# Three of eight pairs of ff tiles of one input stage computed by seven block products

## The chip, the core and the metric

The kernel runs on one core of a Trainium2 chip. The metric is the device time of that core in microseconds, from the start of a launch to its end; below, times without a unit are microseconds. The engines named are PE (TensorE, which does the matmuls, with its own weight loads), DVE (VectorE), ACT (ScalarE) and POOL (GpSimd). SP issues DMA transfers, and POOL issues some too.

## The reference

Two computations follow each other. First, attention over 4 batches, 8 heads, 768 positions, head dimension 64: each query sees the keys less than 16 positions away, and besides them 24 summary keys, the maximum over each block of 32 keys, whose values are the means of the blocks.

```
k_sum = k.reshape(B, H, nb, block, D).max(axis=3)      # block = 32, nb = 24
v_sum = v.reshape(B, H, nb, block, D).mean(axis=3)
scores_all = concat(where(|i - j| < 16, scale * q @ k.T, -1e9), scale * q @ k_sum.T + log(block))
a = softmax(scores_all);  attn = a @ concat(v, v_sum)
```

Second, its output, laid out as 3072 tokens of 512 features, goes through a two-layer network with 2048 hidden features:

```
h = x @ w_in                            # (3072 x 512) @ (512 x 2048)
g = h * (1 / (1 + exp(-1.702 * h)))
out = g @ w_out                         # (3072 x 2048) @ (2048 x 512)
```

## The kernel before

The four batches are handled one after another, each as two halves of 384 tokens, u = 2b and 2b + 1. For the batches b = 1, 2 and 3 the main loop has two stages.

In the *input stage*, PE multiplies the transposed tokens xT with w_in. A hidden feature tile ("ff tile") has 128 of the 2048 features, so that there are 16 in each half, or 8 pairs. A plain ff tile is four matmuls of 128 x 384 (one for each 128 of the 512 input features) into one PSUM tile; ACT takes the tile through the gelu into gT, the operand of the next stage. The profile names these matmuls `ph<-xT,w_in_sb`.

In the *output stage*, gT is multiplied with w_out. Six token tiles of the batch are taken as three pairs a, b and c (class `Pair`, from line 855), and each pair is computed as a 2 x 2 block product with seven products in place of eight (a scheme of the Strassen and Winograd kind), p1 to p7. It needs sums of the blocks of gT (`sums`, three two-input operations on DVE over up to eight pairs of ff tiles; the second one overwrites block a21, which p7 reads as its weights) and sums of w_out's blocks, made once. The products stand in an order written out by hand: p1 of a, then a7, a2, a6, b1, a5, b7, a3, a4, b6, b2, b5, c1, b3, c7, c6, c2, c5, b4, c3, c4. A table, `meets`, says behind which product a step of the next batch's attention (scores, values, transposes of its output) is put. Between the products, `held` copies a PSUM tile to an SBUF tile t, and DVE adds give rows of the output, which SP stores.

Batch 3, the last, also uses seven products in its *input* stage, for the last five of its eight pairs of ff tiles (`ff_in_pairs`, line 702). There the 2 x 2 blocks are the two ff tiles of a pair and two halves of the 512 input features on the side of w_in (a11 to a22), and the halves of the input features and the two halves of the tokens on the side of xT (b11 to b22). A product M1 to M7 is two matmuls of 128 x 384, so that a pair takes 14 matmuls instead of 16. The products accumulate in PSUM: M1's result is copied into Y (line 737), where M2 is added, while its own place X receives M6, M5 and M3 in turn; M7's is held in SBUF (tile m7) and added by DVE to what M6 and M5 leave. Y[0] and Y[1] are the two halves of one PSUM tile, `big[0]`; L, the place of plain tiles (`plain`, line 773) in between, is in `big[1]`. The sums of w_in's blocks (`win_weights`, line 689, four DVE operations for each pair, tile wsum) are made during batch 2's input stage, and those of xT (four operations of 128 x 768, tile xsum) at the start of the last stage.

Every engine issues its instructions in the order in which the program writes them: a helper (line 28) keeps it, and for that reason all rows of the profile name line 28 and are told apart by their tiles. The input stages of batches 1 and 2 also carry work for the next batch, hung behind numbered ff tiles in the tables `first` and `second` (the loop from line 1150): the transposing DMAs on SP's queue that bring keys (kx) and queries (qT); `rest_k`, which reduces the keys to block maxima (ks) and copies halos and maxima into the key rows kx; `v_odd` (line 143), copies within the value rows; `bring`, which computes block sums of the values on PE (ps_vs), copies them (vs), and issues four halo and two sum DMAs on POOL's queue; and `pairs[...].sums`.

Of the kernel before, what the change touches and what calls it, by code (L numbers as in the profile page):

```python
# [35 lines left out]
def kernel(  # L36
# [103 lines left out]
            pool.dma_start(out=w5[:, j, 0, :, 0:D],  # L140
                           in_=v[b, :, j * 128:(j + 1) * 128].rearrange("h p d -> p h d"))

    def v_odd(b):
        for p in range(NP):
            r = rows_of(b % 2, p)
            dve.tensor_copy(out=r[:, :, 1], in_=r[:, :, 0])

    ident = consts.tile([128, 128], BF16, name="ident")
    make_identity(nc, ident)
# [233 lines left out]
    def key_rows(p, s, ks, eng=dve, j0=0):  # L383
        flat = flat_kx(p, s)
        n = NJ - j0
        eng.tensor_copy(out=at(flat, 256 * j0 + 64, [[256, n], [64, 2], [1, nb]]),
                        in_=ks.unsqueeze(1).unsqueeze(1).to_broadcast([128, n, 2, nb]))
# [196 lines left out]
                     in_=rows["q", b][:, 2 * g:2 * g + 2].rearrange("p i j h d -> p (i j h d)"),  # L584
                     transpose=True)

    def rest_k(p, s):
        ks = attp.tile([128, nb], BF16, name="ks", tag="ks")
        dve.tensor_reduce(out=ks.rearrange("p (j e n) -> p j e n", e=2, n=2),
                          in_=at(flat_kx(p, s), 0, [[256, NJ], [192, 2], [block, 2], [1, block]]),  # L590
                          axis=AX.X, op=ALU.max)
        key_halos(p, s)
        key_rows(p, s, ks)

    def tq1(p, eng):
        copy(eng, qT[p][1], trans(rows["q", 1][:, p].rearrange("p j h d -> p j (h d)")))
# [17 lines left out]
    def mask_now():  # L614
        while due:
            due.pop(0)()
# [69 lines left out]
    WI = 5  # L686
    wt = {}

    def win_weights(i0, i1):

        if i0 == 0:
            w = w_in_sb.rearrange("p k (i e c) -> p e k i c", e=2, c=128)[:, :, :, NI - WI:]
            wt.update({(e, h): w[:, e, 2 * h:2 * h + 2] for e in range(2) for h in range(2)})
            wt["s"] = stage.tile([128, 4, 2, WI, 128], F16, name="wsum", tag="kf")
        o, i = [wt["s"][:, n, :, i0:i1] for n in range(4)], slice(i0, i1)
        a11, a12, a21, a22 = (wt[e, h][:, :, i] for e in range(2) for h in range(2))
        dve.tensor_add(o[0], a21, a22)
        dve.tensor_sub(o[1], o[0], a11)
        dve.tensor_sub(o[2], a11, a21)
        dve.tensor_sub(o[3], a12, o[1])  # L700

    def ff_in_pairs(u, early):

        (b11, b21), (b12, b22) = xTT
        xs = castp2.tile([128, 4, 2, HALF], F16, name="xsum", tag="kb")
        t = [xs[:, m] for m in range(4)]
        big = [psb.tile([128, 1024], F32, name="pw_in", tag="big") for _ in range(2)]
        mm = [pmm.tile([128, 512], F32, name="px_in", tag="mm") for _ in range(4)]
        X, V = ([m[:, 0:HALF] for m in mm[n:n + 2]] for n in (0, 2))
# [12 lines left out]
        def prod(ps, a, b, i, first=False):  # L722
            for k in range(2):
                pe.matmul(out=ps, lhsT=a[:, k, i], rhs=b[:, k], start=(first and k == 0),
                          stop=(k == 1), skip_group_check=True)

        ws = [wt["s"][:, n] for n in range(4)]
        hold = {}

        def f0(i):  # L730
            return 2 * (NI - WI + i)

        def M1(i):
            x = X[i % 2]
            prod(x, wt[0, 0], b11, i, True)
            dve.tensor_copy(out=Y[i % 2], in_=x)

        def M7(i):
            v = V[i % 2]
            prod(v, ws[2], t[2], i, True)  # L740
            hold[i] = attp.tile([128, HALF], F32, name="m7", tag="x2")
# [24 lines left out]
        def M3(i):  # L766
            x = X[i % 2]
            prod(x, ws[3], b22, i)
            gelu(u + 1, f0(i), x)

        n, rest = 2 * (NI - WI), list(range(2 * (NI - WI)))

        def plain():
            one(u + 1, rest.pop(0), L)

        for f, ps in zip(range(n), (Y[0], X[1], V[1], L, Y[1], X[1])):
            if f == 2:
                M1(0)
            one(u, f, ps)
        dve.tensor_sub(t[2], b22, b12)  # L780
        dve.tensor_add(t[1], t[2], b11)
        dve.tensor_sub(t[0], b12, b11)
        dve.tensor_sub(t[3], b21, t[1])
        M2(0)
        M7(0)
        M6(0)
        plain()
        for i in range(1, WI):
            M1(i)
            for f in (M7, M5) if i == 1 else (M5, M7):  # L790
                f(i if f is M7 else i - 1)
            M4(i - 1)
            M6(i)
            M3(i - 1)
            M2(i)
            plain()
            if i == 2:
                early(0, NI - WI)
        i = WI - 1
        M5(i)  # L800
        M4(i)
        early(NI - WI, NI)
        plain()
        M3(i)
        assert not rest
# [277 lines left out]
    for u in range(2):  # L1083
# [31 lines left out]
        for i, (ms, part) in enumerate(order):  # L1115
# [6 lines left out]
            if u == 1 and i == 3:  # L1122
                for g in range(2):
# [8 lines left out]
                 "b5": ["x1"], "c1": ["S0", "S1"], "c6": ["S2", "S3"], "c2": ["V0"],  # L1132
                 "c5": ["X0"], "b4": ["V1", "X1"]}}

    def attend(b, what):
        half, i = int(what[0].isupper()), int(what[1])
        kind = what[0].lower()
        if kind == "s":
            scores(b, half, i, True)
            if what == f"S{NP - 1}":  # L1140
                gelu_soon()
        elif kind == "v":
            values(b, half, i, True)
        else:
            dx(i, half)

    for b in range(1, B):
# [17 lines left out]
        if more:  # L1165
            first.setdefault(6, []).append(lambda: v_odd(n))
            at_k = [(first, 3), (first, 5), (first, 8), (first, 10)] if b == 1 else \
                [(first, 8), (first, 10), (first, 12), (first, 14)]
            for p, (when, nt) in enumerate(at_k):
                when.setdefault(nt, []).append(lambda p=p: rest_k(p, s))  # L1170

            def bring():
# [12 lines left out]
            if n + 1 < B:  # L1185
                second[7].append(later)
            when = 7 if b == 1 else 14
            first.setdefault(when, []).append(lambda: [xq(g, n) for g in range(2)])
            first.setdefault(11 if b == 1 else 15, []).append(bring)
        if b == B - 2:  # L1190
            for n0 in range(WI):
                first.setdefault(n0, []).append(lambda n0=n0: win_weights(n0, n0 + 1))
        if not more:
            ff_in_pairs(u, pairs["a"].sums)
        for w, todo in ((u, first), (u + 1, second)) if more else ():
            ff_in(w, range(3))
            for nt in range(NT):
                if nt > 2:
                    ff_in(w, (nt,))
                for f in todo.get(nt, ()):  # L1200
                    f()
        pairs["a"].p1(act)
        if more:
            exp_soon()
        if more:
# [41 lines left out]
```

The softmax here doesn't subtract the row's maximum and nothing guards it: scores larger than these inputs give would overflow.

## Time and profile before

| | us |
|---|---|
| median of 8 runs | 207.48 |
| lowest and highest of the runs | 206.96, 208.3 |
| the profiled execution | 207.39 |
| its span, first to last instruction | 205.7 |
| batch 1: output stage begins | 97.22 |
| batch 2: input stage | 119.67 to 141.13 |
| batch 2: output stage | 141.13 to 163.94 |
| batch 3: input stage | 163.94 to 183.58 |

The profile is of one execution. Its span is the time from the first to the last instruction, and the profiled execution's own time is 1.69 longer. The page gives each engine's busy time, its share in 40 slices, the chain of work that ended last (followed back from the last instruction), and groups of instructions: engine, operation, output tile, input tiles, shape, count, then busy time, mean nanoseconds of one, and the idle time before them with what ended it. The trace behind the page answers for any stretch: a line of a timeline gives start, duration, engine, line, operation, tiles, count, and in brackets the idle time before it and what released it. The stages' bounds in the table are read from the chain, in order of time.

### The profile page before, as it was taken

The numbers are of one execution on the slowest core, as the hardware profiler recorded it, in microseconds if no ns is written. First come the engines' busy times: TensorE is split into PE (matmuls) and PEld (weight loads), VectorE is DVE, ScalarE is ACT, GpSimd is POOL, SyncE is SP. The second block draws the span as 40 slices with busy tenths as digits, with TensorE's granted clock in tenths as the row PEclk, the third lists the DMA queues.
The fourth block names the chain that finished last, engine by engine and source line by source line (L and its number), as shares of the span: only waits on it lengthen the run. The fifth ranks groups of instructions, "written<-read, shape, count | busy, mean of one in ns | idle before, by whom it ended". The sixth has DMA issues, their size and how long they took to land.

```text
span 205.7 us, 5570 instructions
## 1 busy us (share of the span) xinstructions
PE 199.3 (97%) x2212; PEld 136.8 (66%) x2212; DVE 143.7 (70%) x419; ACT 125.0 (61%) x237; POOL 92.0 (45%) x162
## 2 busy tenths in 40 slices
PE   7998999999999999999999999999999999999992
PEld 3866565456655566556888865567887855568882
DVE  5676946697775769766757688589885956669431
ACT  2586675756575589677643657677626477881220
POOL 5995989399898953536999100301000000000000
PEclk9999999999999999999999999999999999999999
DMA  5999999999999999999999997993043260000323
GB/s 176 298 163 207 236 258 219 177 148 230 157 143 183 120 137 179 168 135 156 118 126 203 138 270 144 128 168 59 3 132 101 50 183 0 3 2 26 105 77 102
DMA packets 95009, 28.94 MB, mean 141 GB/s; under 512 B 82880, under 2 KB 92000, under 8 KB 94984
## 3 DMA queue, kind: packets, MB, share of 16 engines
q0 software_dynamic: 67920, 14.88, 81.5%
q1 hardware_dynamic: 25432, 12.53, 30.8%
q10 hardware_dynamic: 1632, 1.18, 1.9%
q8 instruction: 17, 0.28, 0.6%
q14 instruction: 8, 0.07, 0.1%
HBM read 27.26 MB, written 6.29 MB: 163 GB/s over the span
## 4 chain that ended last, share of the span: by engine, by line
PE 83%; DMA 13%; POOL 2%; ACTq 0%; DVE 0%; issue 0%
PE ph L28 26%; PE px L28 16%; PE po L28 10%; DMA w_out_sb<-in_moe_w_out_dram 8%; PE pw L28 8%; PE px_in L28 6%; PE py L28 4%; PE pw_in L28 4%; PE ps_av L28 3%; PE ps_s L28 3%; DMA qf<-in_q_dram 3%; DMA kf<-in_k_dram 2%; PE ps_t L28 1%; POOL w_in_sb L28 1%; PE ps_x L28 1%; PE ps_vs L28 1%
## 5 line engine op out<-in xcount | busy, mean ns | idle before, releaser
L28 PE MATMUL ph<-xT,w_in_sb 128*128 128x384 f16 x384 | 65.2, 326 | 0.1
L28 PEld LDWEIGHTS <-w_in_sb 128*128 128x128 f16 x462 | 44.3, 98 | 28.9 <-issue 0.7
L28 ACT ACTIVATE gT<-ph 128x384 f16<-128x384 f32 x96 | 45.7, 491 | 19.5 <-PE ph L28 19.3
L28 PEld LDWEIGHTS <-gT 128*128 128x128 f16 x384 | 36.0, 98 | 12.1 <-DMA w_out_sb<-in_moe_w_out_dram 0.5
L28 ACT ACTIVATE a_sb<-ps_s 128x768 bf16<-128x768 f32 x28 | 21.1, 806 | 9.5 <-PE ps_s L28 9.5
L28 PE MATMUL po<-w_out_sb,gT 128*128 128x512 f16 x96 | 23.6, 380 | 0.3 <-DMA w_out_sb<-in_moe_w_out_dram 0.3
L28 PEld LDWEIGHTS <-ss 128*128 128x128 f16 x216 | 20.7, 98 | 2.6
L28 ACT ACTIVATE t<-px 128x256 f32<-128x256 f32 x21 | 8.1, 384 | 21.8 <-PE px L28 21.8
L28 DVE TENSOR_TENSOR a_sb<-a_sb,mk 128x768 bf16<-128x768 bf16 x28 | 15.1, 555 | 6.3 <-ACT a_sb L28 5.3
L28 PE MATMUL px<-ta,ss 128*128 128x256 f16 x144 | 18.7, 273 | 0.0
L28 PE MATMUL pw<-tb,gT 128*128 128x256 f16 x144 | 18.7, 273 | 0.0
L28 DVE TENSOR_TENSOR x<-ps_av,rc 128x384 f16<-128x384 f32 x28 | 15.6, 558 | 1.0
L28 POOL DMA_DIRECT2D vw<-in_v_dram x18 | 15.8, 926 | 0.0
L28 POOL DMA_DIRECT2D kb<-in_k_dram x16 | 13.2, 851 | 3.6 <-DMA w_out_sb<-in_moe_w_out_dram 3.2
L28 ACT ACT_TABLE_LOAD x10 | 12.8, 1283 | 3.1 <-issue 2.9
L28 POOL DMA_DIRECT2D vw<-vw x12 | 6.8, 589 | 16.9 <-DVE vw L28 15.3
L28 POOL DMA_DIRECT2D qb<-in_q_dram x16 | 13.3, 909 | 1.7 <-DMA vw<-in_v_dram 1.7
L28 DVE TENSOR_TENSOR osb<-pw,t 128x256 f32<-128x256 f32 x18 | 7.5, 422 | 9.0 <-PE pw L28 5.3
L28 PEld LDWEIGHTS <-kx 64*128 64x128 bf16 x400 | 7.2, 94 | 5.0 <-issue 4.0
L28 DVE TENSOR_REDUCE ks<-kx 128x24 bf16<-128x768 bf16 x8 | 7.6, 946 | 3.8 <-DMA kx<-kb 3.8
L28 DVE TENSOR_TENSOR ss<-gT 128x384 f16<-128x384 f16 (+4 forms) x18 | 7.5, 418 | 3.7 <-ACT gT L28 3.7
L28 POOL DMA_DIRECT2D kq<-in_q_dram x8 | 6.6, 838 | 7.3 <-DMA vw<-in_v_dram 7.2
(120 smaller groups left out, 314.6 us busy)
## 6 DMA issues: line engine op xcount, KB each, us to landing
out_dram<-osb SPq DMA_DIRECT2D x18, 256.0 KB, 4.5
vw<-in_v_dram POOLq DMA_DIRECT2D x18, 128.0 KB, 6.8
w_in_sb<-in_moe_w_in_dram POOLq DMA_DIRECT2D x4, 512.0 KB, 10.6
w_out_sb<-in_moe_w_out_dram POOLq DMA_DIRECT2D x4, 512.0 KB, 20.1
kb<-in_k_dram POOLq DMA_DIRECT2D x16, 96.0 KB, 5.3
qb<-in_q_dram POOLq DMA_DIRECT2D x16, 96.0 KB, 7.3
out_dram<-osb SPq DMA_DIRECT2D x12, 128.0 KB, 1.7
vw<-vs POOLq DMA_DIRECT2D x6, 148.5 KB, 4.3
```

Of the source, the lines that this page charges most:

```text
L28: r = f(*a, **kw)
```

## The change

In batch 2 (b == B - 2) the input stage now does the last three of the eight pairs of ff tiles by the seven products (PB = 3). `ff_in_pairs` is made more general for it: it takes the number of pairs, the tiles for the sums of xT, the list of plain tiles to put between the products, and whether it is the last batch.

- The first half does 10 plain ff tiles, the second 3; then `ff_in_pairs` begins with two plain tiles of the second half into Y[0] and Y[1], then M1(0), M7(0), a plain tile, M2(0), M6(0), a plain tile, and the turns.
- M1's copy into Y is made by ACT in batch 2 (by DVE in the last batch, as before), and m7 takes its SBUF place from the tag a_sb instead of x2.
- The sums of xT for batch 2 are made behind ff tile 8 of the first half. In batch 3 they are where they were.
- The sums of w_in's blocks for pairs 2, 3 and 4 (of five) are made in batch 1's output stage, two operations behind each of b1, b7, a3, c7, c6 and c2; those for pairs 0 and 1 stay at the start of batch 2's input stage.
- v_odd goes from behind ff tile 6 to 2, `bring` from 15 to 6, `rest_k` from 8, 10, 12 and 14 of the first half to 9 of the first, 0 of the second and the first two turns, with its halo and row copies on POOL instead of DVE (the reduction stays on DVE). The queries' transposes xq go from 14 of the first half to 2 of the second.
- The sums for the output stage: a's go from the start of the second half to behind M4 of the last pair; b's from behind tiles 7 and 13 to the end of the stage (pairs 0 to 4) and behind a's p1 (5 to 7); c's from the same places to behind b2 in the output stage, in one piece.

```diff
-    def v_odd(b):
+    def v_odd(b, eng=dve):
         for p in range(NP):
             r = rows_of(b % 2, p)
-            dve.tensor_copy(out=r[:, :, 1], in_=r[:, :, 0])
+            eng.tensor_copy(out=r[:, :, 1], in_=r[:, :, 0])
...
-    def rest_k(p, s):
+    def rest_k(p, s, eng=dve):
         ks = attp.tile([128, nb], BF16, name="ks", tag="ks")
         dve.tensor_reduce(out=ks.rearrange("p (j e n) -> p j e n", e=2, n=2),
                           in_=at(flat_kx(p, s), 0, [[256, NJ], [192, 2], [block, 2], [1, block]]),
                           axis=AX.X, op=ALU.max)
-        key_halos(p, s)
-        key_rows(p, s, ks)
+        key_halos(p, s, eng)
+        key_rows(p, s, ks, eng)
...
-    def win_weights(i0, i1):
-
-        if i0 == 0:
+    def win_weights(i0, part):
+
+        if not wt:
             w = w_in_sb.rearrange("p k (i e c) -> p e k i c", e=2, c=128)[:, :, :, NI - WI:]
             wt.update({(e, h): w[:, e, 2 * h:2 * h + 2] for e in range(2) for h in range(2)})
             wt["s"] = stage.tile([128, 4, 2, WI, 128], F16, name="wsum", tag="kf")
-        o, i = [wt["s"][:, n, :, i0:i1] for n in range(4)], slice(i0, i1)
+        i = slice(i0, i0 + 1)
+        o = [wt["s"][:, n, :, i] for n in range(4)]
         a11, a12, a21, a22 = (wt[e, h][:, :, i] for e in range(2) for h in range(2))
-        dve.tensor_add(o[0], a21, a22)
-        dve.tensor_sub(o[1], o[0], a11)
-        dve.tensor_sub(o[2], a11, a21)
-        dve.tensor_sub(o[3], a12, o[1])
-
-    def ff_in_pairs(u, early):
-
+        if part == 0:
+            dve.tensor_add(o[0], a21, a22)
+            dve.tensor_sub(o[1], o[0], a11)
+        else:
+            dve.tensor_sub(o[2], a11, a21)
+            dve.tensor_sub(o[3], a12, o[1])
+
+    def x_sums(t):
         (b11, b21), (b12, b22) = xTT
-        xs = castp2.tile([128, 4, 2, HALF], F16, name="xsum", tag="kb")
-        t = [xs[:, m] for m in range(4)]
+        dve.tensor_sub(t[2], b22, b12)
+        dve.tensor_add(t[1], t[2], b11)
+        dve.tensor_sub(t[0], b12, b11)
+        dve.tensor_sub(t[3], b21, t[1])
+
+    def ff_in_pairs(u, P, t, rest, last, early):
+
+        (b11, b21), (b12, b22) = xTT
+        hold_tag = "x2" if last else "a_sb"
...
+                pe.matmul(out=ps, lhsT=a[:, k, WI - P + i], rhs=b[:, k], start=(first and k == 0),
...
         def M1(i):
             x = X[i % 2]
             prod(x, wt[0, 0], b11, i, True)
-            dve.tensor_copy(out=Y[i % 2], in_=x)
+            copy(dve if last else act, Y[i % 2], x)
...
+            hold[i] = attp.tile([128, HALF], F32, name="m7", tag=hold_tag)
...
+        if last:
+            for f, ps in zip(range(2 * (NI - P)), (Y[0], X[1], V[1], L, Y[1], X[1])):
+                if f == 2:
+                    M1(0)
+                one(u, f, ps)
+            x_sums(t)
+            M2(0)
+            M7(0)
+            M6(0)
+        else:
+            for y in Y:
+                one(u + 1, rest.pop(0), y)
+            M1(0)
+            M7(0)
+            plain()
+            M2(0)
+            M6(0)
         plain()
-        for i in range(1, WI):
+        for i in range(1, P):
             M1(i)
             for f in (M7, M5) if i == 1 else (M5, M7):
                 f(i if f is M7 else i - 1)
@@ -794,12 +809,11 @@
             M3(i - 1)
             M2(i)
             plain()
-            if i == 2:
-                early(0, NI - WI)
-        i = WI - 1
+            early(i)
...
+        i = P - 1
         M5(i)
         M4(i)
-        early(NI - WI, NI)
+        early(P)
...
+    also_w = ["b1", "b7", "a3", "c7", "c6", "c2"]
...
+            ts_x = []
+
+            def sums_x():
+                ts_x.extend(attp.tile([128, 2, HALF], F16, name="xs", tag="x2") for _ in range(4))
+                x_sums(ts_x)
+
+            first = {0: [lambda: win_weights(0, 0), lambda: win_weights(0, 1)],
+                     1: [lambda: win_weights(1, 0), lambda: win_weights(1, 1)],
+                     2: [lambda: v_odd(n)], 6: [bring], 8: [sums_x],
+                     9: [lambda: rest_k(0, s, pool)]}
+            second = {0: [lambda: rest_k(1, s, pool)],
+                      2: [lambda: [xq(g, n) for g in range(2)]]}
+
+            def also(i):
+                if i < PB:
+                    rest_k(i + 1, s, pool)
+                if i == PB:
+                    pairs["a"].sums(0, NI)
+
+        def also_last(i):
+            if i == 2:
+                pairs["a"].sums(0, NI - WI)
+            elif i == WI:
+                pairs["a"].sums(NI - WI, NI)
+
         if not more:
-            ff_in_pairs(u, pairs["a"].sums)
+            xs = castp2.tile([128, 4, 2, HALF], F16, name="xsum", tag="kb")
+            ff_in_pairs(u, WI, [xs[:, m] for m in range(4)], range(2 * (NI - WI)), True, also_last)
         for w, todo in ((u, first), (u + 1, second)) if more else ():
+            ends = (NT, NT) if b < B - 2 else (2 * (NI - PB), 2 * (NI - PB) - 4 - PB)
             ff_in(w, range(3))
-            for nt in range(NT):
+            for nt in range(ends[w - u]):
                 if nt > 2:
                     ff_in(w, (nt,))
                 for f in todo.get(nt, ()):
                     f()
+        if b == B - 2:
+            ff_in_pairs(u, PB, ts_x, range(2 * (NI - PB) - 4 - PB, 2 * (NI - PB)), False, also)
+            pairs["b"].sums(0, NI - PB)
...
+        if b == B - 2:
+            pairs["b"].sums(NI - PB, NI)
+        elif more:
...
+            if b == 1 and what in also_w:
+                win_weights(2 + also_w.index(what) // 2, also_w.index(what) % 2)
+            if b == B - 2 and what == "b2":
+                pairs["c"].sums(0, NI)
```

More of the change, by code (lines that the diff above doesn't have):

```diff
@@ L723, in prod @@
             for k in range(2):
-                pe.matmul(out=ps, lhsT=a[:, k, i], rhs=b[:, k], start=(first and k == 0),
+                pe.matmul(out=ps, lhsT=a[:, k, WI - P + i], rhs=b[:, k], start=(first and k == 0),
                           stop=(k == 1), skip_group_check=True)
@@ L730, in f0 @@
         def f0(i):
-            return 2 * (NI - WI + i)
+            return 2 * (NI - P + i)
         def M1(i):
@@ L740, in M7 @@
             prod(v, ws[2], t[2], i, True)
-            hold[i] = attp.tile([128, HALF], F32, name="m7", tag="x2")
+            hold[i] = attp.tile([128, HALF], F32, name="m7", tag=hold_tag)
             copy(act, hold[i], v)
@@ L769, in M3 @@
             gelu(u + 1, f0(i), x)
-        n, rest = 2 * (NI - WI), list(range(2 * (NI - WI)))
+        rest = list(rest)
         def plain():
             one(u + 1, rest.pop(0), L)
[L776 to L786, printed above, removed]
+        if last:
[15 more added lines that the diff above has]
+            M6(0)
         plain()
-        for i in range(1, WI):
+        for i in range(1, P):
             M1(i)
@@ L1170 @@
                 when.setdefault(nt, []).append(lambda p=p: rest_k(p, s))
+            PB = 3
             def bring():
@@ L1190 @@
         if b == B - 2:
-            for n0 in range(WI):
-                first.setdefault(n0, []).append(lambda n0=n0: win_weights(n0, n0 + 1))
+            ts_x = []
[18 more added lines that the diff above has]
+                pairs["a"].sums(NI - WI, NI)
         if not more:
-            ff_in_pairs(u, pairs["a"].sums)
+            xs = castp2.tile([128, 4, 2, HALF], F16, name="xsum", tag="kb")
+            ff_in_pairs(u, WI, [xs[:, m] for m in range(4)], range(2 * (NI - WI)), True, also_last)
         for w, todo in ((u, first), (u + 1, second)) if more else ():
+            ends = (NT, NT) if b < B - 2 else (2 * (NI - PB), 2 * (NI - PB) - 4 - PB)
             ff_in(w, range(3))
-            for nt in range(NT):
+            for nt in range(ends[w - u]):
                 if nt > 2:
@@ L1204 @@
             exp_soon()
-        if more:
+        if b == B - 2:
+            pairs["b"].sums(NI - PB, NI)
+        elif more:
             for m in "bc":
```

## The prediction

> **What bounds the kernel now.** I read four views. First the page's busy table and slices:
>
> ```profile
> span 205.7 us, 5570 instructions
> ...
> PE 199.3 (97%) x2212; PEld 136.8 (66%) x2212; DVE 143.7 (70%) x419; ACT 125.0 (61%) x237; POOL 92.0 (45%) x162
> ...
> PEclk9999999999999999999999999999999999999999
> ```
>
> PE (TensorE) has 3% of idle time and its clock is granted in full in every slice, so PE time saved is time saved, unless a wait appears. Second, the chain that ended last, in order of time, around batch 2's input stage (119.67 to 141.13) and the head of its output stage:
>
> ```profile
> 119.67 10.51 PE ph L28 x64
> 130.18 0.45 PE ps_vs L28 x24
> 130.63 10.51 PE ph L28 x64
> 141.13 0.87 PE px L28 x8
> 142.01 0.87 PE pw L28 x8
> 142.88 0.46 PE ps_s L28 x24
> ...
> 156.05 0.87 PE pw L28 x8
> 156.92 0.87 PE px L28 x8
> ```
>
> Everything is PE with no gap between its pieces. The price of a matmul follows: 10.51 / 64 = 0.164; a run of four takes 0.65 elsewhere in this chain, so 0.1625 each and 0.11 once per stretch. Third, the groups of instructions by form: what feeds and drains PE.
>
> ```profile
> L28 ACT ACTIVATE gT<-ph 128x384 f16<-128x384 f32 x96 | 45.7, 491 | 19.5 <-PE ph L28 19.3
> L28 DVE TENSOR_REDUCE ks<-kx 128x24 bf16<-128x768 bf16 x8 | 7.6, 946 | 3.8 <-DMA kx<-kb 3.8
> L28 DVE TENSOR_TENSOR wsum<-w_in_sb 128x256 f16<-128x256 f16 x10 | 2.9, 285 | 0.0
> L28 DVE TENSOR_TENSOR ss<-gT 128x1024 f16<-128x1024 f16 x4 | 2.7, 677 | 0.0
> ```
>
> A gelu of one ff tile lasts 0.49; a two-input add over all eight pairs lasts 0.68. Fourth, the time table of the last stage, which already uses seven products, and of VectorE (DVE) where batch 2's sums go today:
>
> ```profile
> core 0: us, PE busy (x) PEld busy (x) DVE busy (x) ACT busy (x) POOL busy (x), PEclk, DMA share, GB/s
> 119.67:141.13 21.46, 21.46 (x156) 12.88 (x155) 17.25 (x61) 14.79 (x31) 3.51 (x6) 1.00 1.04 164
> 163.94:183.58 19.64, 19.64 (x120) 11.55 (x119) 12.04 (x25) 15.32 (x36) 0.00 (x0) 1.00 0.19 54
> ```
> ```profile
> 153.46 0.68 DVE L28 TENSOR_TENSOR ss<-gT,ss 128x1024 f16<-128x1024 f16 x1
> 154.06 0.42 DVE L28 TENSOR_TENSOR osb<-py,t 128x256 f32<-128x256 f32 x1
> 154.40 0.41 DVE L28 TENSOR_TENSOR osb<-pw,t 128x256 f32<-128x256 f32 x1
> 154.73 0.41 DVE L28 COPY t<-px 128x256 f32<-128x256 f32 x1
> 155.78 1.26 DVE L28 TENSOR_TENSOR a_sb<-a_sb,mk 128x768 bf16<-128x768 bf16 x2 [0.64 <-ACT a_sb L28]
> ```
>
> The last stage's 118 input matmuls would take 118 x 0.1625 = 19.18 and take 19.64: five pairs of the scheme lost 0.46 to waits, where ten matmuls (1.63) were saved. In the second table c1's copy of t ends at 155.14, and the sum before it is one operation.
>
> **The change, part by part.** In both directions the count is on PE; "later" means later than today's time of the same instruction.
>
> 1. *Removed.* Three pairs, each 14 matmuls instead of 16: 6 x 0.1625 = **-0.98**.
>
> 2. *The first two tiles of the scheme.* In the second half the first plain tiles go to Y[0] and Y[1], the two halves of one PSUM tile. The built program's PE queue holds a wait there: the second one's first matmul waits for ScalarE's (ACT's) gelu of the first. The last stage puts other tiles between its two. Y[0]'s last matmul ends at 119.67 + 56 x 0.1625 + 0.45 + 2 x 0.11 = 129.44. Then hand-over 0.04, gelu 0.49, hand-over 0.05, and a first matmul that shows its full 0.326 of the group ph<-xT instead of 0.163: **+0.74**. Nothing can cover it: PE runs in order, and M1(0) and all that follows stand behind it. Bounds 0.4 (only what the 0.49 leaves after the pipelined drain) and 0.8.
>
> 3. *The rest of the scheme.* The L tile is written again while its own gelu is pending (0.12 in the first turn, 0.07 at the tail), and M3(0) waits for VectorE's add (0.16; the last stage shows 0.17 of idle between its M4 and M3): **+0.35**. Bounds 0.2 and the last stage's whole 0.46.
>
> 4. *a's sums.* Today they are spread over the second half. Now all eight pairs go in one piece behind M4(2)'s gelus, and a7's weights (the second sum's output) wait for them. From M4's end: gelu 0.49, hand-over 0.04, two sums 0.71 and 0.69, hand-over and weight load 0.15: about 2.1. PE has a plain tile, M3 and a's p1 meanwhile: 1.76. **+0.3** (0.1 to 0.4). b's sums follow behind and are needed two products later; they are covered.
>
> 5. *c's sums.* Today c's are done mostly in the input stage. Now three operations of 0.68 (1.9 in sequence) stand on VectorE behind b2, ahead of b5's output add and of c1's copy of t. From the rows above, that copy ends 1.9 later, 155.14 to 157.05; c6 stands in PE's queue at 156.76, after the table's shift, and needs it: **+0.34**. Bounds 0 (0.64 of idle follows the copy, but the copy is before it) and 0.7.
>
> 6. *Edits that cost nothing.* Twelve operand sums of weights in batch 1's output stage: 0.285 each, some 0.5 for each two, in VectorE's gaps before 103.47, 106.24 and 112.72; without that cover 0.5 at one place. Value rows earlier, the vsum matmuls earlier: same count of PE. ScalarE gets three M1 copies and three holds, 6 x 0.39 = 2.3 on 14.79 of 21.46: room. Key rows move from VectorE to POOL, 4 x 0.6 to POOL, and are due at the scores (142.9 and 146): covered by more than 5. The x sums, four of 0.555, start when xT is in place and end near 128.1; M7(0) reads them after 131: covered by 3.
>
> 7. *What is moved on queues.* Four halo and two sum DMAs move on POOL's queue from 128 to 139 to about 125 to 129, so that they lie beside the kx transposes on SP's queue, whose order is unchanged. VectorE's two pairs of key reductions wait for kx (idle 1.36 and 2.46 today), and now stand ahead of the scheme's adds in its queue. The first kx lands at about 129.3 and the adds are needed at 131.8; the second 134.4 against 136.6. So 2.2 of lateness is hidden; beyond it each us costs one us. Taken: 0. Bounds 0 and +2.
>
> *A rule that speaks against point 6.* The x sums have two SBUF inputs and POOL issues DMAs beside them. The Trainium skill ("SBUF — State Buffer", section "SBUF: two separate sides") says that such a VectorE operation and a GpSimd operation hold one port pair exclusively in turn. The row first:
>
> ```profile
> 95.03 6.64 POOL L28 DMA_DIRECT2D kb<-in_k_dram  x8 [0.39 <-issue]
> ...
> 142.32 0.35 DVE L28 TENSOR_TENSOR ss<-gT 128x384 f16<-128x384 f16 x1
> ```
>
> The same add beside that POOL stretch, at 96.48, lasted 0.36; with POOL idle, 0.35. By the rule the sums would wait behind six issues of about 0.55 and end at 128.1 + 3.3 = 131.4, a stall of about 0.4 at M7(0), so 208.7 in all. By the row nothing. I take the row. No row shows a POOL *copy* beside such adds at this place; that is part of the range.
>
> **The sum.** -0.98 + 0.74 + 0.35 + 0.30 + 0.34 = +0.75. The profiled execution took 207.39 around a span of 205.7 (1.69 outside it, unchanged); so 208.14 and a span of 206.45. The median, 207.48, lies 0.09 above the profiled one: 208.23, told as **208.3** since points 4 and 5 were rounded down (2.12 - 1.76 is 0.36).
>
> **The rivals.**
>
> *A: Y[1] is not held up.* If the wait on the first gelu costs nothing (it is met early, or the order on the chip hides it), point 2 goes and the sum is +0.01: 207.5, no change. For it: the last stage has the same PSUM tile and no visible stop there. Against: there an L tile, X and V lie between. It decides from a wait under 0.3.
>
> *B: kx comes late.* The moved DMAs slow the transposes. In batch 1 the qT transposes with halos and sums beside them took 7.95 for two, in batch 2 5.49. If the second kx lands 3.5 later instead of 2.2, the reduction holds the adds of turn 1 by 1.3: 208.3 + 1.3 = 209.6. For it also: the DMA share of this stretch is 1.04 in the table above, full. Against: today's halos already lie beside the second kx (they start at 128.25), so only the two sum DMAs are new to it. Decides from 2.2 of lateness.
>
> *C, the other side: the stage loses only what the last stage lost.* That is the measured cost of this scheme, 0.46, for five pairs; if all of Y, L and M3 waits come to 0.3 to 0.46, and VectorE's one-piece sums find their gaps as today's do, the gain stays: -0.98 + 0.46 = -0.52, 207.0; at best 206.5. Place: the input stage's end; it decides if all waits of points 2 to 5 together are under 0.56. For it: that stage is measured, and my waits are read from a queue. Against: its sums were split, its Y tiles apart.
>
> **How the numbers follow.** A change under 0.2% (0.41) cannot be told from none here. Likeliest, as worked out: 0.60, own range 207.9 to 208.8. A: 0.15. B: 0.14. C: 0.11. Slower by over 0.2% (above 207.9) takes B and nearly all of the likeliest, less what falls in its lower end, 0.02: 0.72. Same: A and that lower end, less 0.01 that A spreads to the fast side: 0.16. Faster (below 207.07): C and that 0.01: 0.12. Range: below 207.3 lies most of C (0.09), above 209.3 most of B (0.10); so 207.3 to 209.3.
>
> **What would show it.** Right: the stretch between the first ph matmul of batch 2 and the end of its a7 becomes some 0.4 to 0.5 longer, not 0.98 shorter; a PE gap of 0.5 to 0.6 before Y[1]'s first matmul, released by ACT; gaps of about 0.15 before M3; a gap of 0.3 before a7 and of 0.3 before c6, both released by VectorE. The stages ahead of 119.67 and behind 163.94 keep their lengths. Wrong: no gap at Y[1] (A), a gap in turn 1 behind a key reduction that waits for kx (B), or a batch-1 output stage that grows because the twelve weight sums push an output add back.

## The result

The changed kernel takes 208.6 (median of 20 runs), the kernel before 207.5 (57 runs). The ratio of their times is 1.0043, with a 95% interval of 1.0027 to 1.0059, that is 0.56 to 1.22 slower. A later series of the changed kernel gave 208.41 against 207.27, ratio 1.0030 (1.0008 to 1.0051). The forecast was 208.3, slower, and its sum was +0.75.

The profile that came with the result is of an execution of 212.66 (span 210.9), one of the few that are longer than the others at a lower mean granted clock (0.992 here); the ratios and intervals in this document leave those out, the medians do not. I call it the long execution. It shows one mechanism at its largest; an ordinary execution (208.62) follows under the first experiment. From the page of the long one, busy table, slices and chain:

```profile
span 210.9 us, 5571 instructions
...
PE 199.8 (95%) x2206; PEld 135.2 (64%) x2206; DVE 145.5 (69%) x404; ACT 126.4 (60%) x243; POOL 96.0 (46%) x178
...
PEclk9999999999999999999999999969999999999999
...
PE 56%; DMA 25%; POOL 9%; DVE 4%; issue 3%; SPq 1%; ACT 0%; POOLq 0%; DVEq 0%
```

The six matmuls are gone (2206 against 2212), but PE's share fell, and the chain no longer runs through PE alone in batch 2: it enters the input stage through a transposing DMA of the keys. PE's timeline of the same execution has these idle stretches (the bracket is the idle time before the row and what ended it):

```profile
130.76 0.81 PE L28 MATMUL pw_in<-xT,w_in_sb 128*128 128x384 f16 x4 [0.58 <-ACT gT L28]
...
137.21 0.64 PE L28 MATMUL px_in<-xs,wsum 128*128 128x384 f16 x2 [2.30 <-DVE px_in L28]
...
147.01 1.05 PE L28 MATMUL pw<-tb,gT 128*128 128x256 f16 x8 [0.17 <-DVE gT L28]
...
162.30 1.03 PE L28 MATMUL px<-ta,ss 128*128 128x256 f16 x8 [0.21 <-DVE t L28]
```

The first, third and fourth are at the three places of the prediction's points 2, 4 and 5, each released by the engine named there. A gap costs about 0.16 more than the bracket says, since the first matmul behind a stop shows its whole length (0.326 of 128 x 384, where 0.1625 is the price of one in a row). The second gap, the largest, is rival B. SP's queue and VectorE say where it comes from; the first row is the kernel before's, the second the long execution's:

```profile
123.66 6.23 SPq L28 DMA_TRANSPOSE kx<-kb  x4
124.92 9.50 SPq L28 DMA_TRANSPOSE kx<-kb  x4
```
```profile
134.75 1.81 DVE L28 TENSOR_REDUCE ks<-kx 128x24 bf16<-128x768 bf16 x2 [4.65 <-DMA kx<-kb]
136.59 0.57 DVE L28 TENSOR_TENSOR px_in<-px_in,m 128x384 f32<-128x384 f32 x1
```

The four key transposes occupy SP's queue for 9.50 instead of 6.23. That row is the time in which they are issued; from issue to landing they take a median of 9.5 each, before 4.8. VectorE idles 4.65 for them, makes two reductions (1.81), and only then the first turn's add (px_in), for which PE has been waiting. (A turn is the stretch of the scheme in which one pair is finished and the next one begun.)

To compare stages apart from the start of an execution, which varies (batch 2's input stage begins between 118.96 and 120.72 in the fourteen profiles), I use one number below, *the period*: from the first matmul of batch 2's input stage to the first of batch 3's, both from the chain in order of time. Before: 119.67 to 163.94, 44.27; a second execution of the kernel before: 118.96 to 163.22, 44.26. The long execution above: 120.42 to 169.47, 49.05. Batch 1's output stage, which got the twelve sums of weights, lasts 22.45 in both kernels (97.22 to 119.67, and 97.97 to 120.42).

One thing outside the period also changed. From the end of the last output add to the end of the span the kernel before takes 3.2 to 3.3 (205.7 - 202.45 in its first profile), and so does `before_early` below; every kernel with the scheme in batch 2 takes 2.9 to 3.0, some 0.3 less (206.9 - 203.94 in the ordinary execution). The prediction had nothing there, and no run shows the cause. For these kernels a longer period should thus make the whole time longer by 0.3 less.

### The profile page after: what moved, and what is told of

Read it like the earlier page. It is cut to its first block, busy times and chain, and to the rows that moved or that the text cites. A ratio compares the mean times of both kernels' runs of the same rounds, so it can differ in the third digit from the quotient of the medians.

```text
span 210.9 us, 5571 instructions
## 1 busy us (share of the span) xinstructions
PE 199.8 (95%) x2206; PEld 135.2 (64%) x2206; DVE 145.5 (69%) x404; ACT 126.4 (60%) x243; POOL 96.0 (46%) x178
## 4 chain that ended last, share of the span: by engine, by line
PE 56%; DMA 25%; POOL 9%; DVE 4%; issue 3%; SPq 1%; ACT 0%; POOLq 0%; DVEq 0%
PE px L28 13%; PE ph L28 12%; DMA w_out_sb<-in_moe_w_out_dram 10%; PE px_in L28 8%; PE pw L28 7%; PE pw_in L28 5%; DMA kx<-kb 4%; DMA w_in_sb<-in_moe_w_in_dram 4%; PE py L28 4%; POOL qb L28 3%; DMA kq<-in_k_dram 3%; PE ps_av L28 2%; POOL vw L28 2%; PE ps_s L28 2%; PE po L28 2%
## 5 line engine op out<-in xcount | busy, mean ns | idle before, releaser
L28 PEld LDWEIGHTS <-w_in_sb 128*128 128x128 f16 x432 | 41.7, 98 | 28.8 <-issue 3.1
L28 PE MATMUL ph<-xT,w_in_sb 128*128 128x384 f16 x308 | 52.8, 326 | 0.2
L28 ACT ACTIVATE gT<-ph 128x384 f16<-128x384 f32 x77 | 36.4, 491 | 16.2 <-PE ph L28 16.0
L28 PE MATMUL pw_in<-xT,w_in_sb 128*128 128x384 f16 x80 | 16.2, 335 | 0.6 <-ACT gT L28 0.6
L28 ACT ACTIVATE gT<-pw_in 128x384 f16<-128x384 f32 x24 | 11.4, 492 | 4.0 <-PE pw_in L28 3.7
L28 ACT ACTIVATE gT<-px_in 128x384 f16<-128x384 f32 x19 | 9.3, 490 | 4.6 <-PE px_in L28 4.4
L28 PEld LDWEIGHTS <-wsum 128*128 128x128 f16 x64 | 6.5, 101 | 7.3 <-issue 3.4
```

Of the source, the lines that this page charges most:

```text
L28: r = f(*a, **kw)
```

## The experiments

Two theories. Theory 1 is the prediction's: the waits at Y[1], at a7 and at c6 make the loss. Theory 2 is its rival B as the usual case: the six early DMAs make the keys late, and the reductions carry that lateness to the adds.

### The changed kernel once more

> The changed kernel as it is, for a profile of another execution. The profile at hand shows one in which kx landed at 134.66 and PE stood still for 2.30 behind VectorE's reductions. Theory 1 (the waits of the prediction's points 2 to 5 make the loss, late keys are an accident of some executions): time 208.3 to 208.8; where no late kx disturbs, gaps on PE of 0.58 at Y[1], about 0.17 before a7 and 0.2 before c6, first kx by 131.5, and nothing behind the key reductions. Theory 2 (rival B is the usual case: the moved halo and sum DMAs make kx late): a gap of 0.3 or more behind a VectorE add in the first turn, with kx landing after 132.

The median is 208.41, the ratio 1.0030; this profiled execution took 208.62. PE's timeline:

```profile
129.45 0.81 PE L28 MATMUL pw_in<-xT,w_in_sb 128*128 128x384 f16 x4 [0.58 <-ACT gT L28]
...
138.75 0.48 PE L28 MATMUL px_in<-xT,wsum 128*128 128x384 f16 x2 [1.09 <-DVE c L28]
...
142.96 1.05 PE L28 MATMUL pw<-tb,gT 128*128 128x256 f16 x8 [0.17 <-DVE gT L28]
...
158.25 1.03 PE L28 MATMUL px<-ta,ss 128*128 128x256 f16 x8 [0.20 <-DVE t L28]
```

and VectorE around the second of these, with the same reduction in the kernel before put first:

```profile
134.45 0.95 DVE L28 TENSOR_REDUCE ks<-kx 128x24 bf16<-128x768 bf16 x1 [2.46 <-DMA kx<-kb]
```
```profile
137.28 0.95 DVE L28 TENSOR_REDUCE ks<-kx 128x24 bf16<-128x768 bf16 x1 [2.04 <-DMA kx<-kb]
138.15 0.55 DVE L28 TENSOR_TENSOR c<-px_in,m 128x384 f32<-128x384 f32 x1
```

The period is 119.11 to 165.43: 46.32. Both theories' gaps are there. The first keys come just in time here (the reductions start at 130.62, the add behind them at 132.47), but the second keys are at VectorE 18.17 after the stage's start (137.28 - 119.11), where before they were there after 14.78 (134.45 - 119.67): 3.39 later. That reduction holds the second turn's c, and PE loses 1.09. The transposes occupied SP's queue for 8.54 and landed a median of 9.5 after issue.

### Taking away the two waits, singly and together

`y_apart` removes the wait at Y[1]:

```diff
-            for y in Y:
+            for y in (Y[0], X[1]):
```

> The scheme's second plain tile goes to X[1] instead of Y[1], in another PSUM tile than the first; nothing else. Theory 1: the wait on the first gelu goes, with the 0.58 of idle and the 0.16 of the exposed first matmul: 0.74 less than the changed kernel, so about 207.9, close to the kernel before. Theory 2: PE then only comes to the late adds earlier and waits there longer: 208.3 to 208.7, and the gap behind the adds grows by 0.7.

`dma_late` moves only the six DMAs, which POOL issues, to behind the third plain tile of the second half:

```diff
                 block_sums()
-                halo_dmas(w5, 0)
-                sum_dmas(w5, 0)
+                if b == 1:
+                    send()
+
+            def send():
+                w5 = vw[s].rearrange("p (j e) h c -> p j e h c", e=2)
+                halo_dmas(w5, 0)
+                sum_dmas(w5, 0)
...
-                      2: [lambda: [xq(g, n) for g in range(2)]]}
+                      2: [lambda: [xq(g, n) for g in range(2)], send]}
```

> The four halo and two sum DMAs are issued behind the third plain tile of the second half instead of behind tile 6 of the first; their matmuls and copies stay. On POOL's queue they thereby stand behind the key copies of the first two head pairs. Theory 1: the median stays within 0.2 of the changed kernel's (the waits remain), only the few long executions go. Theory 2: kx lands by 130 to 131 and the median falls by 0.4 or more, to 208.2 or less, with a narrower spread.

`y_dma` has both edits.

> Both edits together. Theory 1: 207.9, as the first edit alone. Theory 2: at most 207.5, more than the two edits' gains alone would add up to, since each hides the other's wait.

The two kernels with X[1] leave out the plain tile that Y[1] holds before M1's copy goes there. They do not compute the reference's output and serve for timing alone; the number and shape of the instructions are the changed kernel's.

| kernel | median | ratio to before (95%) | period of the profiled execution |
|---|---|---|---|
| changed, first series | 208.6 | 1.0043 (1.0027 to 1.0059) | 49.05 |
| changed, second series | 208.41 | 1.0030 (1.0008 to 1.0051) | 46.32 |
| y_apart | 208.56 | 1.0043 (1.0020 to 1.0066) | 45.93 |
| dma_late | 207.87 | 1.0017 (0.9991 to 1.0042) | 45.07 |
| y_dma | 207.41 | 0.9990 (0.9967 to 1.0013) | 44.33 |

Theory 1 expected y_apart 0.74 faster than the changed kernel. It is not: the median is no lower. Its profile shows why. The gap at Y[1] is gone, and PE, earlier by that much, stands twice behind VectorE instead:

```profile
134.54 0.48 PE L28 MATMUL px_in<-xs,wsum 128*128 128x384 f16 x2 [0.47 <-DVE px_in L28]
139.57 0.48 PE L28 MATMUL px_in<-xT,wsum 128*128 128x384 f16 x2 [0.81 <-DVE c L28]
```

Its period is 0.39 shorter than in the ordinary execution of the changed kernel, and its second keys came 0.38 earlier (17.79 after the stage's start instead of 18.17). From the reduction of the second keys to the period's end it is 28.14 here (138.10 to 166.24), and 28.15 with the wait at Y[1] in place (137.28 to 165.43). So in these two executions the second keys alone set the period, and the wait at Y[1] is hidden in front of them.

Once the DMAs are late, removing the same wait does pay: the period falls from 45.07 to 44.33, by exactly the 0.74 of point 2. And with the Y wait gone, moving the DMAs takes 1.0043 to 0.9990; the two intervals do not touch. In dma_late the keys are as quick as in the kernel before (a median of 4.0 from issue to landing), and of the gaps the three of the prediction remain:

```profile
123.88 6.24 SPq L28 DMA_TRANSPOSE kx<-kb  x4
```
```profile
130.15 0.81 PE L28 MATMUL pw_in<-xT,w_in_sb 128*128 128x384 f16 x4 [0.58 <-ACT gT L28]
...
142.41 1.05 PE L28 MATMUL pw<-tb,gT 128*128 128x256 f16 x8 [0.17 <-DVE gT L28]
...
157.70 1.03 PE L28 MATMUL px<-ta,ss 128*128 128x256 f16 x8 [0.20 <-DVE t L28]
```

Its period, 45.07, is 0.80 above the kernel before's. That is the prediction's sum (+0.75), measured without rival B.

A second series of the same kernel:

> The kernel with the late DMAs again, for a second interval (the first was 0.9991 to 1.0042, the changed kernel's 1.0008 to 1.0051 and 1.0027 to 1.0059). By the stage alone (period 45.07 against 44.27) 0.8 slower than before: ratio 1.0039. If the kernel before loses something to late keys too, less: 1.002.

The median is 207.96 against 207.27, the ratio 1.0030 (1.0009 to 1.0050), the period 45.07 again (119.05 to 164.12). The 0.80, less the 0.3 at the end, would be a ratio of 1.0024, which lies between the two series. In the comparison of times dma_late (1.0017, 1.0030) and the changed kernel (1.0043, 1.0030) are not told apart with certainty: how much the late keys cost the changed kernel in its usual executions stays open between nothing and about 0.5. In its two profiled executions it was 1.25 (46.32 - 45.07) and 3.98, the latter with 1.84 for a low clock (last section).

### The early DMAs alone, and twice

`before_early` is the kernel before with the early value rows and DMAs:

```diff
-            first.setdefault(6, []).append(lambda: v_odd(n))
+            first.setdefault(6 if b == 1 else 2, []).append(lambda: v_odd(n))
...
-            first.setdefault(11 if b == 1 else 15, []).append(bring)
+            first.setdefault(11 if b == 1 else 6, []).append(bring)
```

> The kernel before, with the value rows behind tile 2 and the block sums of the values with their six DMAs behind tile 6 of the first half, as in the changed kernel; nothing of the scheme. If the moved DMAs are what slows the key transposes, the four take 8 to 9.5 instead of 6.2 here too, and as no add stands behind the reductions, the period stays 44.27 and the time is that of the kernel before within 0.3. If the lateness comes from something else in the changed kernel: 6.2.

The transposes occupy SP's queue for 8.51 and land a median of 8.4 after issue, so the lateness needs no block scheme in this stage; that it is the DMAs, and not the value rows moved with them, dma_late has shown. But the expectation for the time was wrong: 208.17 against 207.47, ratio 1.0023 (1.0006 to 1.0041), and the period is 45.08 (119.54 to 164.62). I had held that no add stands behind the reductions in this kernel. The sums of the pairs do. VectorE in the kernel before, then VectorE and PE in before_early:

```profile
138.14 0.67 DVE L28 TENSOR_TENSOR ss<-gT 128x1024 f16<-128x1024 f16 x1
```
```profile
137.06 0.95 DVE L28 TENSOR_REDUCE ks<-kx 128x24 bf16<-128x768 bf16 x1 [2.11 <-DMA kx<-kb]
137.93 0.37 DVE L28 COPY kx<-kx 128x80 bf16<-128x80 bf16 x3
138.22 0.23 DVE L28 COPY kx<-ks 128x288 bf16<-128x288 bf16 x1
138.36 0.95 DVE L28 TENSOR_REDUCE ks<-kx 128x24 bf16<-128x768 bf16 x1
...
139.65 0.68 DVE L28 TENSOR_TENSOR ss<-gT 128x1024 f16<-128x1024 f16 x1
```
```profile
148.89 1.05 PE L28 MATMUL px<-w_out_sb,ss 128*128 128x256 f16 x8 [0.51 <-DVE ss L28]
```

a's sums start at 139.65 instead of 138.14, all later sums follow without a gap, and nine microseconds on PE waits 0.51 for one of them. That costs 0.67; with 0.14 lost at the product before, it is the 0.81 by which the period is longer.

`twice` is the changed kernel with the DMAs doubled at their early place:

```diff
-                halo_dmas(w5, 0)
-                sum_dmas(w5, 0)
+                for _ in range(1 if b == 1 else 2):
+                    halo_dmas(w5, 0)
+                    sum_dmas(w5, 0)
```

> The changed kernel with the four halo and two sum DMAs issued twice at their early place (the second time the same bytes to the same rows); nothing else. If a late kx, through the reductions ahead of the adds, is what the early DMAs cost, twice the bytes make kx 1 to 3 later and the gap behind the adds as much wider: 209.5 to 211.5. If the lateness seen in the profiles has little to do with the usual time: 208.3 to 208.7, like the changed kernel.

The median is 212.14 (four runs, 208.81 to 214.08), the ratio 1.0131 (1.0073 to 1.0188). That is longer than expected (209.5 to 211.5), but the profile does not show the expected cause. In the profiled execution (210.83) the key transposes occupy the queue for 8.42, no longer than in the ordinary execution, and the second keys are at VectorE 18.80 after the stage's start (139.52 - 120.72), later by 0.63 and not by 1 to 3. The period, 46.95, is longer by the same 0.63; from the second keys to its end it is again 28.15. Most of the 2.21 by which this execution is longer (210.83 - 208.62) lies ahead of the stage, which begins 1.61 later (120.72, 119.11), where the edit changes nothing. So the run shows once more that the second keys set the period; that more early DMAs cost more is not shown by four runs.

### The reductions later in VectorE's queue

```diff
-                     2: [lambda: v_odd(n)], 6: [bring], 8: [sums_x],
-                     9: [lambda: rest_k(0, s, pool)]}
-            second = {0: [lambda: rest_k(1, s, pool)],
-                      2: [lambda: [xq(g, n) for g in range(2)]]}
+                     2: [lambda: v_odd(n)], 6: [bring], 8: [sums_x]}
+            second = {2: [lambda: [xq(g, n) for g in range(2)]]}
...
-                    rest_k(i + 1, s, pool)
+                    rest_k(i - 1, s, pool)
                 if i == PB:
                     pairs["a"].sums(0, NI)
+                    rest_k(2, s, pool)
+                    rest_k(3, s, pool)
```

> The DMAs early as in the changed kernel, so kx as late as there, but the key reductions stand later in VectorE's queue: the first behind the first turn, the second behind the second, the other two behind a's sums. If it is the reductions' place ahead of the adds that turns a late kx into PE time, the gap behind the adds goes although kx lands 8.5 or later after its issue began, and the median falls by about 0.5 against the changed kernel, to 207.9. If the early DMAs cost in another way (the transposes of the queries, the value rows), no change: 208.5.

The trace is as expected: the transposes occupy the queue for 9.47, and PE has no gap behind the adds. A gap of 0.17 behind a sum appears later (`px<-w_out_sb,ss`), since two reductions now stand ahead of b's sums. The period is 45.40. The median is not as expected: 208.52, ratio 1.0039 (1.0020 to 1.0058), no better than the changed kernel.

> A second execution of the kernel with the early DMAs and the later reductions, whose median did not fall although no gap before the adds was seen. If in usual executions kx comes later still, a gap of 0.3 or more returns behind the reduction of the first or second turn; if not, the period is 45.4 as in its first profile.

The second execution again has the period 45.40, transposes of 8.75 and no gap behind the adds, and took 207.7. So a late key costs PE nothing at the adds when no add stands behind the reduction: that holds in two executions. The first of the two took 208.48; the difference lies ahead of the stage, which begins at 119.91 and at 119.10.

The median fits this period: 45.40 is 1.13 above the kernel before's, and 1.13 less the 0.3 at the end is a ratio of 1.0040. What did not fit was the expectation, which took the changed kernel's loss from its profiles. Its period of 46.32, less 0.3, would be a ratio of 1.0084; its measured ones are 1.0030 and 1.0043. So its usual executions, by this estimate from medians, lose some 0.1 to 0.4 to late keys (0.62 to 0.89, with the 0.3 put back and the 0.80 of dma_late's period taken off), much less than its two profiled ones. That is about what reduce_spread still loses (45.40 - 45.07 = 0.33).

The kernel before, in another execution:

> The kernel before in another execution, for how much its own key transposes and its batch 2 period (44.27, four transposes in 6.23) vary. If late keys touch it too: transposes over 7 and a PE gap in the output stage behind sums; otherwise 6.2 to 6.5 and 44.3.

It took 206.7. The transposes occupy the queue for 5.76, the period is 44.26, and there is no gap: the keys are no later than in its first profile.

### The sums in pieces, and all mends together

`sums_apart` is dma_late with

```diff
+            first.setdefault(9, []).insert(0, lambda: pairs["a"].sums(0, NI - PB))
...
-                    pairs["a"].sums(0, NI)
+                    pairs["a"].sums(NI - PB, NI)
...
-            if b == B - 2 and what == "b2":
-                pairs["c"].sums(0, NI)
+            if b == B - 2 and what in ("b1", "b2"):
+                pairs["c"].sums(*((0, 4) if what == "b1" else (4, NI)))
```

> Late DMAs and the two sums in pieces, with Y[0] and Y[1] filled one after the other as in the changed kernel. By points 4 and 5: no idle before a7 and c6, period 45.07 - 0.6 = 44.45. If another VectorE operation takes their place: 45.0.

The period is 44.36 (119.92 to 164.28): 0.71 less than dma_late's. The gaps before a7 and c6 are gone and nothing takes their place; 0.58 at Y[1] is the one that is left. The one run took 207.49.

`mended` is sums_apart with a tile between the two Y tiles, for which the second half does one plain tile fewer ahead of the scheme; the queries' transposes and the six DMAs go behind the second of its two tiles:

```diff
-            for y in Y:
+            for y in (Y[0], L, Y[1]):
...
-                      2: [lambda: [xq(g, n) for g in range(2)]]}
+                      1: [lambda: [xq(g, n) for g in range(2)], send]}
...
-            ends = (NT, NT) if b < B - 2 else (2 * (NI - PB), 2 * (NI - PB) - 4 - PB)
-            ff_in(w, range(3))
+            ends = (NT, NT) if b < B - 2 else (2 * (NI - PB), 2 * (NI - PB) - 5 - PB)
+            ff_in(w, range(min(3, ends[w - u])))
```

> Four edits: the halo and sum DMAs late as in the third kernel run; a plain tile in L between those in Y[0] and Y[1] (one fewer ahead of the scheme), so that nothing waits for the first gelu; a's sums for the five plain pairs behind tile 9 of the first half, for the other three behind M4; c's sums in two pieces, behind b1 and behind b2. Period from the first matmul of batch 2's input stage to that of batch 3's: before 44.27, changed kernel with late DMAs 45.07. If the waits add up as in the prediction's points 2, 4 and 5 (0.74, 0.3, 0.3), the period is 45.07 - 1.3 = 43.75 and the median 0.5 under the kernel before. If the waits only move on to the next late operation, it stays at 44.3, with no gain.

The median is 206.54 against 207.47, the ratio 0.9948 (0.9931 to 0.9966): faster than both kernels. The period as one window in the kernel before, in dma_late and in mended:

```profile
119.67:163.94 44.27, 44.27 (x516) 32.08 (x515) 36.03 (x113) 27.49 (x54) 3.51 (x6) 1.00 0.64 112
```
```profile
119.81:164.88 45.07, 44.12 (x508) 31.29 (x508) 35.73 (x86) 28.84 (x60) 7.73 (x22) 1.00 0.62 109
```
```profile
119.96:163.68 43.72, 43.72 (x509) 31.45 (x508) 36.52 (x92) 28.84 (x60) 7.88 (x22) 1.00 0.70 117
```

The columns are the stretch, its length, then busy time and count of PE, weight loads, VectorE, ScalarE and POOL, the granted clock, the DMA share and GB/s. In dma_late PE is idle for 0.95 of 45.07; in mended it counts as busy throughout. The period is 0.55 under the kernel before: of the 0.98 saved, the scheme's small waits keep 0.43. They are too short to show as idle, but the starts of the matmuls show them: 0.09 among the three first tiles (twelve matmuls take 2.04 where 1.95 would do), 0.165 ahead of M3(0), and 0.085 and 0.095 ahead of two L tiles.

## Why the prediction was right, and where not

The forecast, 208.3 and slower, was right, and the waits that it named are there at their sizes. That the time came so close is in part luck: two things that it had at nothing, the late keys and the end of the span, have opposite signs.

- *What bounds the kernel.* Right: PE is busy throughout the period in the kernel before (44.27 of 44.27) and in mended (43.72 of 43.72), and what the edits took off its waits came off the period.
- *Point 1, -0.98.* Six matmuls fewer. In mended the period is 0.55 shorter and the waits left are 0.435 by the starts of the matmuls, together 0.985.
- *Point 2, Y[1], +0.74.* The gap is 0.58, released by ACT, and its removal takes 0.74 off the period (45.07 to 44.33), when nothing else is late. "Nothing can cover it" is wrong where the keys are late: PE then waits for them further on, and the same removal showed nothing in the median.
- *Point 3, +0.35.* It measured 0.355 in dma_late. M5's two matmuls begin at 134.78, so that M3's could at 135.105; they begin at 135.27, 0.165 late. The L tiles behind the pairs of matmuls at 132.42 and 139.82 begin at 132.84 and 140.24, 0.095 late each.
- *Points 4 and 5, a7 and c6, 0.30 + 0.34.* Together 0.71 (45.07 to 44.36), both where they were put and released by VectorE. With them the sum closes: -0.98 + 0.74 + 0.355 + 0.71 is 0.825, where 0.80 was measured.
- *Point 6, at nothing.* Right for the weight sums (22.45 in both), the x sums and the copies of M1. In the ordinary execution POOL issues DMAs from 124.87 to 128.30, the x sums begin at 126.67, and they last 0.55 to 0.56, as in dma_late (0.54 to 0.56), where POOL issues nothing beside them: the row was right for DMA issues. The section that the prediction set against it (the Trainium skill, "SBUF — State Buffer", section "SBUF: two separate sides") has operations with two SBUF inputs contend only with a GpSimd operation that reads SBUF, a condition that the prediction left out.
- *Point 7, DMAs, taken at 0.* This is the step that failed. The key transposes occupy SP's queue for 8.4 to 9.5 in all six profiled executions that keep the changed kernel's early DMAs, and 8.51 with them in the kernel before, against 5.76 to 6.50 in the seven without; from issue to landing it is a median of 8.1 to 9.5 against 4.0 to 5.0. The lateness of the second keys, 3.39, is over the 2.2 of slack; rival B had put 1.3 on 3.5 of lateness, and the ordinary profile shows 1.25. It was given 14 in 100 as an alternative to the sum; it is an addition to it, met in both profiles of the changed kernel. Against it I had said that today's halos already lie beside the second keys. They do, but not beside the first, which were 1.87 later too (11.51 after the stage's start, before 9.64) and stand ahead of the second in SP's queue. What it is in the six DMAs that slows the transposes is not shown.
- *The stages behind 163.94.* They were to keep their lengths. The span's end is 0.3 nearer to the last add, which no point had.

So the forecast hit the time because four of its terms were near their size, and because the late keys (nothing to 0.5 in usual executions) and the shorter end (-0.3) about cancel.

## What to carry to other kernels

One wait can hide another on the same engine: remove two suspects singly and together, since one alone may show nothing. When a DMA is moved earlier, look up which other transfers are then under way, and follow the queue of the engine that waits for the slowed transfer: what matters is which instruction stands behind that wait. A saving of six matmuls needs every wait it brings to be smaller; here four small reorderings turned 0.3 to 0.4% slower into 0.5% faster.

## What the runs showed of the hardware

A stop of TensorE can be followed by a stretch at half clock. In the long execution PE idled 2.30, up to 137.21. The windows before and after the stop, and a later one (columns as above, so that the granted clock is third from the end):

```profile
131.40:134.90 3.50, 3.50 (x22) 1.95 (x20) 0.15 (x1) 2.74 (x7) 0.19 (x1) 1.00 1.26 128
137.20:139.90 2.70, 2.69 (x10) 1.27 (x10) 1.22 (x3) 0.99 (x3) 0.24 (x2) 0.54 1.14 159
140.00:143.00 3.00, 3.00 (x18) 1.66 (x17) 1.26 (x2) 2.33 (x6) 1.55 (x6) 0.86 0.87 162
```

0.54 and 0.86 are means over parts of one stretch. In shorter windows the granted clock is 0.50 from about 137.4 to 140.8, and 1.00 on both sides. The chain has eight matmuls in 2.56 at 137.21 and the next six in 1.56, where 14 x 0.1625 = 2.28 would do: 1.84 lost on top of the 2.30. The gaps of 1.09 in the ordinary execution and of 1.21 in twice brought no such loss; the clock of their periods is 1.00. That the stop brings the low clock is read from the order in time in one execution. No run varies the length of a stop, so whether it is the length that decides, and where between 1.21 and 2.30, is not shown.

Copies on POOL and two-input sums on VectorE can take longer when they meet. In both runs with the later reductions a key copy of 128x288 on POOL took 0.69, elsewhere 0.43, and the sum of 128x640 beside it took 0.71, elsewhere 0.48. From the first of the two:

```profile
145.33 0.69 POOL L28 COPY kx<-ks 128x288 bf16<-128x288 bf16 x1
```
```profile
145.66 0.71 DVE L28 TENSOR_TENSOR ss<-ss,gT 128x640 f16<-128x640 f16 x1
```

Just before, three key copies of 128x80 took 1.03, elsewhere 0.73, while the first sum beside them kept its 0.48. So POOL copies beside such sums, which the prediction left to its range, do cost something: 0.2 to 0.3 on either side. In the ordinary execution of the changed kernel the copies do not meet such sums.
